# A linear-attention and token-mixing kernel with forty early warm-up matmuls and a new order of all its steps

## The chip, the cores and the metric

The kernel runs on one core of one Trainium2 chip. Its engines, as this text names them: PE (TensorE, matmuls; PEld is its weight load), DVE (VectorE), ACT (ScalarE), POOL (GpSimd) and SP (SyncE, which issues most DMAs). Each takes its instructions strictly in its own order and waits on semaphores for the others. The metric is the device time of one execution in microseconds (us), as the median of several runs. Before the change it is 267.01 us over three runs (266.68 to 268.0).

## The reference

Eight batches of 576 tokens, 8 heads of 64: a linear attention with cosine weights on relu features, and then a mixer over tokens and over channels.

```python
def _attn_ref(q, k, v):                       # 8 x 8 x 576 x 64
    theta = np.pi / 2.0 * pos / S
    def phi(x, c, s):
        r = np.maximum(x, 0.0)
        return np.concatenate([r * c, r * s], axis=-1)
    q_p, k_p = phi(q, cos_w, sin_w), phi(k, cos_w, sin_w)
    kv = np.einsum('bhsf,bhsd->bhfd', k_p, v)
    z = np.sum(k_p, axis=2)
    num = np.einsum('bhsf,bhfd->bhsd', q_p, kv)
    den = np.einsum('bhsf,bhf->bhs', q_p, z)[..., None] + 1e-06
    return num / den
def _moe_ref(x, w_tok1, w_tok2, w_ch1, w_ch2):   # x: 8 x 576 x 512
    h = np.maximum(x.transpose(0, 2, 1) @ w_tok1, 0.0) @ w_tok2
    u = x + h.transpose(0, 2, 1)
    return u + np.maximum(u @ w_ch1, 0.0) @ w_ch2
```

## The kernel before

The whole kernel is a list of small steps, each a function that issues a few instructions (L259 to L742). The program is written out in full; nothing loops on the chip. A letter in a step names its engine: A is ACT, V is DVE, G is POOL, Y is SP.

*Tokens.* The 576 tokens of a batch lie on 128 partitions, four full tiles (j = 0 to 3) and a half-filled fifth (j = 4). The fifth tiles of two batches make one tail tile; the four tails of all batches are the ninth group (g = 8) of the channel mixer.

*Attention of a batch b.* `load` (L274) brings k, q, v. `feat` and `rfeat` (L299, L293) make the relu features in bf16, `vcast` (L309) the bf16 v with a column of ones. `kv` (L598) multiplies features and v on PE, `kv_out` copies the sum to SBUF. q's features are turned: for batches 0 and 1 by PE transposes (`q_turn_mm` L585, 8 matmuls against the identity, and `q_turn_out`, a copy from PSUM), later by DMA (`q_turn` L318, on SP). `num` (L614) multiplies, `x_out` (L621, three DVE instructions) divides and writes x. Batch 0 is done in two halves of four heads (`kv_half`, `num_half`, `x_half` and `b1_half`, L501 to L565).

*Token mixer.* `b1` (L631, two of five matmuls each) and `b1_out` (relu), `u_mm` (L645, two of four matmuls) and `u_out` (L652, DVE, adds x), `u_cast` to bf16 and `u_turn` (L659), a DMA transpose on SP that makes uT. Batch 0 makes its uT on PE instead (`uT_x`, `uT_h`, `uT_out`, L567 to L583). `tail_mm`, `tail_out` and `tail_turn` do the same for two batches' tails.

*Channel mixer of group g.* `m1` (L690) is one of 12 slices of the first layer, four matmuls of 128x512; it needs all of uT. `m1_out` is its relu from PSUM to h1T. The second layer of group 0 is `m2` (L701, 12 steps of four matmuls of 128x512). From group 1 on it is done in a scheme with seven products of half size in place of eight: `h_sum` (L344) makes sums of h1T slices, `prod` (L716, 12 matmuls of 128x256) multiplies, `seed` copies one PSUM bank, `quarter` (L729, DVE) adds to u, and `store` writes out. `w_sum` makes the matching sums of the second weight.

*PSUM.* `take` and `give` (L392, L397) hand out two tiles of two banks (psA, kind "P") and four of one bank (psM, kind "S") in turn. A step that takes a tile waits for whoever read the one before out of it.

*Weights.* `wtok_load`, `wc1_load`, `wc2_load` (L460, L467, L487) bring f32 weights into buffers that are free at that time, and `w1_cast`, `w2_perm`, `w2t_perm`, `wc1_cast`, `wc2_cast` make bf16 copies of them.

*Warm-up.* `warm(n)` (L493) issues n matmuls of 128x512 on zeros (wz, cleared at L411); nothing reads their result.

*Order.* Every step stands in one of the tables ONCE (L21), BATCH (L79) and GROUP (L154) with a place, a number. L749 to L763 add 19 per batch, sort all steps by place and issue them. So the place sets the order in which each engine sees its instructions, the order of SP's DMAs, and who gets which PSUM tile. Batches 3 to 7 and groups 1 to 7 share rows, with some exceptions.

## Time and profile before

| what | value |
|---|---|
| median of 3 runs | 267.01 us (266.68 to 268.0) |
| span of the profiled execution | 265.7 us |
| PE busy | 245.6 us (92% of the span), 2081 matmuls |
| DVE busy | 186.4 us (70%), 360 instructions |
| ACT busy | 135.5 us (51%), 233 instructions |
| POOL busy | 90.1 us (34%), 109 instructions |
| DMA | 57.70 MB, mean 217 GB/s; 380 to 398 GB/s from 7 to 40 us |
| chain of waits | PE 86%, DMA 6%, DVE 3%, SP's queue 1%, ACT 1%, POOL 1% |

The profile is one execution, taken on the chip. Busy time is the time in which an engine had an instruction under way; matmuls overlap in PE's pipeline, so a matmul is listed as longer (379 ns for 128x512) than the distance between two (216 ns). The chain of waits is followed back from the last instruction to what released it, and so on. Over-busy engines off that chain cost nothing by themselves. The first m1 step starts at 33.13 us, the last matmul ends at 261.3 us. Queue times of DMAs: a load of 640 KB lands a median of 5.5 to 8.2 us after its issue, a DMA transpose of qpT 3.4 us, of uT 3.8 us.

### The profile page before, as it was taken

Reading aid. Unit: us, or ns where it says so; the run is one execution under the profiler, and the core shown is the slowest. Engines: PE = TensorE matmul, PEld = TensorE weight load, DVE = VectorE, ACT = ScalarE, POOL = GpSimd, SP = SyncE. Lnnn points to the kernel's source line nnn. Section 1 sums busy time; section 2 is a strip of 40 time slices with the busy share of each in tenths; the row PEclk is TensorE's granted clock in tenths of the full one; section 3 lists DMA queues with packets and bytes.
Section 4 is the critical chain, followed back from the end, with each engine's and each line's share of the span. In section 5 each row is a group of like instructions: output and inputs, shape, how many; then the busy total and the mean of one; then the engine's idle time right before and its main releaser. Section 6 shows DMA issues by size and latency. Waiting matters only on the chain.

```text
span 265.7 us, 5384 instructions
## 1 busy us (share of the span) xinstructions
PE 245.6 (92%) x2081; PEld 158.7 (60%) x2081; DVE 186.4 (70%) x360; ACT 135.5 (51%) x233; POOL 90.1 (34%) x109
## 2 busy tenths in 40 slices
PE   0198999998999999999999999999999999999993
PEld 0176556554448855775487548754875486486482
DVE  4468888969779879778695868587948384256462
ACT  2547678845754387448636863486324402521300
POOL 5064255609634106420460046006600240130340
PEclk9999999999999999999999999999999999999999
DMA  6999999799999899969999999996972043103004
GB/s 195 393 398 386 382 383 368 252 290 152 284 372 157 188 347 336 160 128 317 345 198 128 293 377 182 134 342 221 157 119 121 0 81 148 34 1 158 2 0 159
DMA packets 81754, 57.70 MB, mean 217 GB/s; under 512 B 50240, under 2 KB 76480, under 8 KB 81728
## 3 DMA queue, kind: packets, MB, share of 16 engines
q1 hardware_dynamic: 80768, 56.31, 76.6%
q10 hardware_dynamic: 960, 1.05, 1.3%
q8 instruction: 16, 0.26, 0.4%
q14 instruction: 10, 0.08, 0.1%
HBM read 35.85 MB, written 9.44 MB: 170 GB/s over the span
## 4 chain that ended last, share of the span: by engine, by line
PE 86%; DMA 6%; DVE 3%; SPq 1%; ACT 1%; issue 1%; POOL 1%; DVEq 0%; POOLq 0%
PE psM L694 35%; PE psM L359 26%; PE psA L637 6%; PE psA L649 5%; DMA uT<-u_bf 3%; PE psA L603 3%; DMA v_raw<-in_v_dram 3%; PE psA L617 3%; PE psM L706 2%; PE psM L496 1%; SPq L272 1%; PE psA L676 1%; PE psA L590 1%; PE psM L506 1%; DVE u_sb L653 1%
## 5 line engine op out<-in xcount | busy, mean ns | idle before, releaser
L694 PE MATMUL psM<-uT,w_ch 128*128 128x512 bf16 x384 | 89.9, 379 | 1.4 <-DMA uT<-u_bf 1.4
L287 ACT ACTIVATE h1T<-psM 128x512 bf16<-128x512 f32 x92 | 51.5, 596 | 55.9 <-PE psM L694 54.1
L694 PEld LDWEIGHTS <-w_ch 128*128 128x128 bf16 x432 | 40.5, 98 | 45.4 <-DMA uT<-u_bf 1.8
L283 POOL CAST vb<-v_raw 128x512 bf16<-128x512 f32 (+1 forms) x30 | 20.0, 698 | 70.5 <-DMA v_raw<-in_v_dram 70.5
L359 PEld LDWEIGHTS <-h1s 128*128 128x128 bf16 x384 | 36.7, 98 | 4.9
L371 DVE TENSOR_TENSOR u_sb<-psM,u_sb 128x512 f32<-128x512 f32 x42 | 28.7, 688 | 15.0 <-PE psM L359 14.7
L348 POOL TENSOR_TENSOR h1s<-h1T,h1s 128x512 bf16<-128x512 bf16 (+1 forms) x16 | 21.1, 1318 | 43.9 <-ACT h1T L287 31.3
L359 PE MATMUL psM<-w_ch2t,h1s 128*128 128x256 bf16 x288 | 34.4, 273 | 0.0
L359 PEld LDWEIGHTS <-h1T 128*128 128x128 bf16 x288 | 27.5, 98 | 4.8
L653 DVE TENSOR_TENSOR u_sb<-psA,x_sb 128x1024 f32<-128x1024 f32 x16 | 19.4, 1220 | 12.7 <-PE psA L649 12.5
L305 ACT ACTIVATE kp<-k_raw,sin_t 128x512 bf16<-128x512 f32 x32 | 22.3, 716 | 7.0 <-DMA k_raw<-in_k_dram 5.0
L359 PE MATMUL psM<-w_ch,h1T 128*128 128x256 bf16 x192 | 23.6, 273 | 0.0
L348 DVE TENSOR_TENSOR h1s<-h1T 128x512 bf16<-128x512 bf16 (+1 forms) x24 | 17.5, 728 | 5.5 <-ACT h1T L287 5.4
L305 ACT ACTIVATE kp<-k_raw,cos_t 128x512 bf16<-128x512 f32 x24 | 16.9, 716 | 6.2 <-PE psA L603 5.9
L627 DVE TENSOR_TENSOR x_sb<-psA,rden 128x512 bf16<-128x512 f32 x28 | 19.4, 691 | 1.0
L289 DVE TENSOR_SCALAR h1T<-psM 128x512 bf16<-128x512 f32 x16 | 10.8, 686 | 10.7 <-PE psM L694 10.4
L590 PE MATMUL psM<-ident,qp 128*128 128x128 bf16 x40 | 4.4, 274 | 12.5 <-ACT qp L287 12.5
L617 PEld LDWEIGHTS <-qpT 128*128 128x128 bf16 x280 | 12.3, 98 | 5.5
L649 PE MATMUL psA<-B,w_tok 128*128 128x512 bf16 x64 | 15.6, 379 | 0.0
L283 POOL CAST u_bf<-u_sb 128x1024 bf16<-128x1024 f32 x7 | 9.5, 1359 | 16.3 <-DVE u_sb L653 14.0
L624 DVE TENSOR_SCALAR rden<-psA,eps_t 128x8 f32<-128x8 f32 x35 | 7.8, 223 | 10.3 <-PE psA L617 9.3
L348 POOL TENSOR_TENSOR h1s<-h1T 128x512 bf16<-128x512 bf16 x8 | 10.1, 1261 | 13.3 <-ACT h1T L287 13.3
(114 smaller groups left out, 342.1 us busy)
## 6 DMA issues: line engine op xcount, KB each, us to landing
out_dram<-u_sb SPq DMA_DIRECT2D x32, 256.0 KB, 7.8
q_raw<-in_q_dram SPq DMA_DIRECT2D x8, 640.0 KB, 5.5
k_raw<-in_k_dram SPq DMA_DIRECT2D x8, 640.0 KB, 7.1
v_raw<-in_v_dram SPq DMA_DIRECT2D x7, 640.0 KB, 8.2
q_raw<-in_q_dram SPq DMA_DIRECT2D x8, 512.0 KB, 4.4
k_raw<-in_k_dram SPq DMA_DIRECT2D x7, 512.0 KB, 6.0
v_raw<-in_v_dram SPq DMA_DIRECT2D x7, 512.0 KB, 7.0
u_sb<-in_moe_w_ch_dram SPq DMA_DIRECT2D x2, 1024.0 KB, 10.1
```

The lines of the kernel that those rows point to most:

```text
L283: eng.tensor_copy(out_ap, in_ap)
L287: eng.activation(out_ap, in_ap, AF.Relu)
L305: eng.activation(dst, src, AF.Relu, bias=0.0, scale=s)
L348: eng.tensor_tensor(out=o[:, k0:k1], in0=a[:, k0:k1], in1=b_[:, k0:k1], op=op)
L359: nc.tensor.matmul(bank[:, t * HC:(t + 1) * HC], lhs[:, ki, t * P:(t + 1) * P], rhs[:, ki, :], start=(first and ki == 0 and t == 0), stop= ...
L371: V.tensor_add(u, bank2(bank)[:, ts, :], u)
L617: nc.tensor.matmul(ps[:, h // HH, (h % HH) * E1:(h % HH + 1) * E1], qpT[:, h, j, :], kv_sb[:, h, 0:E1], start=True, stop=True, skip_group_ ...
L627: V.tensor_mul(dst.rearrange("p (g h d) -> p g h d", g=2, h=HH), n[:, :, :, 0:D], bcast(r, [[HH, 2], [1, HH], [0, D]]))
L637: nc.tensor.matmul(ps[:, mi, :], w1[:, j, mi * P:(mi + 1) * P], rhs, start=(j == 0), stop=(j == NJ - 1))
L649: nc.tensor.matmul(ps[:, half, :], w2[:, ki, 2 * c + half, :], B1[b % 2][:, ki, :], start=(ki == 0), stop=(ki == NT - 1))
L653: V.tensor_add(u_sb[b % 2][:, 2 * c:2 * c + 2, :], of(("u", b, c)), x_sb[:, 2 * c:2 * c + 2, :])
L694: nc.tensor.matmul(ps.rearrange("p (t k) -> p t k", k=P), wc1[:, ki, s * P:(s + 1) * P], src[:, :, ki, :], start=(ki == 0), stop=(ki == NC ...
```

## The change

The tables ONCE, BATCH and GROUP and the sort are replaced by one tuple PLAN that lists all 1032 steps in the order in which they are issued. No step of the computation is dropped or added (eight entries of the old tables that issue nothing, tails of even batches, are not listed any more): the same matmuls, copies and DMAs, with the same shapes, are issued in another order, and some on another engine. The memset of wz moves to the front of DVE's program.

Warm-ups: before, 15 matmuls in two steps (3 behind kv_half(0,1), 12 behind num_half(0,2)). After, 20 steps of two: 17 of them stand before the first transpose of batch 0, one right behind it, one before num_half(1,0) and one before the first m1.

Steps by engine, before and after (only kinds that differ):

| kind | ACT | DVE | POOL |
|---|---|---|---|
| m1_out | 92, 70 | 16, 38 | |
| feat | 75, 62 | 45, 58 | |
| rfeat | 8, 15 | 16, 9 | |
| h_sum | | 40, 37 | 24, 27 |
| vcast and vcast_half | 9, 12 | 6, 12 | 30, 21 |
| u_cast | 3, 7 | 4, 1 | 7, 6 |
| wc1_cast and wc2_cast | 2, 4 | 3, 4 | 19, 16 |
| b1_out, kv_out and their halves | 22, 16 | 3, 9 | |
| x_tail and tail_out (of the four tails) | 1, 2 | 3, 2 | 4, 4 |

SP's loads of the head: before k, q, v of batch 0 with v's first part ahead of q's second, then the last third of w_ch1, w_tok, the second third, k and q of batch 1, the first third, v of batch 1. After: q's second part ahead of v, then w_tok, the second third of w_ch1, k of batch 1, the last third, the first third, q and v of batch 1. Then, before, two thirds of w_ch2, k of batch 2, the last third, v and q of batch 2; after, a third of w_ch2, k, the next third, v, q, the last third.

The core of the diff:

```diff
-ONCE = (
-    (-247.4, "load_part", 0, "k", 0, "Y", 0, 8), (-223.9, "load_part", 0, "q", 1, "Y", 0, 8),
-    (-248.1, "load_part", 0, "q", 0, "Y", 0, 8), (-227.5, "load_part", 0, "v", 1, "Y", 0, 4),
-    (-214.7, "load_part", 0, "v", 0, "Y", 0, 4), (-215.8, "load_part", 0, "v", 1, "Y", 4, 8),
-    (-206.9, "load_part", 0, "v", 0, "Y", 4, 8), (-59.4, "warm", 12), (-131.9, "wtok_load"),
-    (-62.9, "wc1_load", 0, 0, 256), (-74.8, "wc1_load", 0, 256, 512), (-100.1, "wc1_load", 1),
-    (-145.1, "wc1_load", 2), (-152.8, "feat", 0, "k", 0, 0, "A"), (-212.5, "feat", 0, "k", 1, 0, "A"),
...
-    (-113.3, "vcast_half", 1, 4, "G"), (-87.2, "kv_half", 0, 4), (-72.2, "kv_half_out", 0, "A"), (-102.3, "warm", 3),
-    (-63.4, "num_half", 0, 0), (-61.2, "x_half", 0, 0, 0), (-59.9, "x_half", 0, 0, 1), (-55.8, "num_half", 0, 1),
...
-BATCH = {}
...
-GROUP = {}
...
+PLAN = (
+    ("load_part", 0, "q", 0, "Y", 0, 8), ("warm", 2), ("warm", 2), ("load_part", 0, "k", 0, "Y", 0, 8),
+    ("feat", 0, "k", 1, 0, "A"), ("load_part", 0, "q", 1, "Y", 0, 8), ("feat", 0, "k", 1, 2, "A"),
+    ("load_part", 0, "v", 1, "Y", 0, 4), ("feat", 0, "q", 1, 4, "A"), ("rfeat", 0, "q", 2, 4, "A"),
+    ("feat", 0, "k", 0, 2, "V"), ("feat", 0, "k", 0, 0, "V"), ("warm", 2), ("warm", 2), ("rfeat", 0, "q", 0, 2, "V"),
+    ("feat", 0, "q", 1, 1, "V"), ("feat", 0, "q", 1, 0, "V"), ("feat", 0, "q", 1, 3, "A"),
+    ("load_part", 0, "v", 0, "Y", 0, 4), ("load_part", 0, "v", 0, "Y", 4, 8), ("load_part", 0, "v", 1, "Y", 4, 8),
+    ("feat", 0, "k", 0, 4, "V"), ("vcast_half", 0, 4, "V"), ("wtok_load",), ("feat", 0, "q", 1, 2, "V"), ("warm", 2),
+    ("warm", 2), ("vcast_half", 1, 1, "G"), ("warm", 2), ("rfeat", 0, "q", 4, 5, "A"), ("warm", 2), ("wc1_load", 1),
+    ("vcast_half", 1, 4, "A"), ("warm", 2), ("warm", 2), ("feat", 0, "k", 0, 3, "V"), ("warm", 2), ("warm", 2),
+    ("warm", 2), ("warm", 2), ("warm", 2), ("warm", 2), ("warm", 2), ("vcast_half", 1, 2, "G"),
+    ("q_turn_mm", 0, 4, "S"), ("vcast_half", 0, 1, "V"), ("warm", 2), ("feat", 0, "k", 1, 1, "A"),
+    ("q_turn_out", 0, 4, "A", "S"), ("vcast_half", 0, 0, "V"), ("kv_half", 0, 0), ("q_turn_mm", 0, 3, "S"),
+    ("feat", 0, "k", 1, 4, "A"), ("w2_perm", 1, "G"), ("feat", 0, "k", 0, 1, "V"), ("feat", 0, "k", 1, 3, "V"),
+    ("load", 1, "k", "Y"), ("vcast_half", 0, 3, "V"), ("kv_half", 0, 1), ("q_turn_mm", 0, 2, "S"),
+    ("q_turn_mm", 0, 1, "S"), ("vcast_half", 0, 2, "V"), ("kv_half", 0, 2), ("kv_half", 0, 3), ("w1_cast", 4, 5, "G"),
+    ("vcast_half", 1, 3, "A"), ("wc1_load", 2), ("w1_cast", 2, 4, "G"), ("w1_cast", 0, 2, "V"),
+    ("q_turn_out", 0, 3, "V", "S"), ("kv_half", 0, 4), ("kv_half_out", 0, "A"), ("wc1_load", 0, 256, 512),
+    ("q_turn_out", 0, 1, "A", "S"), ("vcast_half", 1, 0, "V"), ("kv_half", 1, 0), ("kv_half", 1, 1),
+    ("q_turn_mm", 0, 0, "S"), ("wc1_cast", 3, "G"), ("wc1_cast", 8, "G"), ("q_turn_out", 0, 0, "V", "S"),
+    ("q_turn_out", 0, 2, "A", "S"), ("w2t_perm", 0, "G"), ("num_half", 0, 0), ("kv_half", 1, 2), ("kv_half", 1, 3),
+    ("kv_half", 1, 4), ("kv_half_out", 1, "A"), ("wc1_load", 0, 0, 256), ("wc1_cast", 0, "G"), ("num_half", 0, 2),
+    ("x_half", 0, 0, 0), ("x_half", 0, 0, 1), ("num_half", 0, 1), ("b1_half", 0, 0), ("num_half", 1, 2),
+    ("x_half", 0, 2, 0), ("x_half", 0, 1, 0), ("x_half", 0, 2, 1), ("x_half", 0, 1, 1), ("warm", 2),
+    ("num_half", 1, 0), ("x_half", 1, 0, 0), ("num_half", 1, 1), ("uT_x", 1), ("b1_half", 0, 1), ("x_half", 1, 0, 1),
+    ("load", 1, "q", "Y"), ("x_half", 1, 1, 0), ("b1_half", 0, 2), ("b1_half", 0, 3), ("x_half", 1, 1, 1),
+    ("x_half", 1, 2, 0), ("x_half", 1, 2, 1), ("wc1_cast", 2, "G"), ("wc1_cast", 6, "G"), ("wc1_cast", 5, "V"),
+    ("load", 1, "v", "Y"), ("wc1_cast", 11, "G"), ("b1_half", 0, 4), ("b1_half", 1, 0), ("feat", 1, "k", 0, 2, "V"),
+    ("b1_half", 1, 1), ("b1_half", 1, 2), ("b1_half", 1, 3), ("b1_half_out", 0, "A"), ("b1_half", 1, 4),
+    ("b1_half_out", 1, "V"), ("w2_perm", 0, "A"), ("uT_h", 1), ("uT_x", 0), ("uT_h", 0), ("uT_x", 2),
+    ("wc1_cast", 9, "G"), ("uT_h", 2), ("uT_out", 0, "A"), ("uT_out", 1, "A"), ("feat", 1, "k", 1, 2, "V"),
+    ("uT_out", 2, "A"), ("u_mm", 0, 1), ("w2t_perm", 1, "A"), ("uT_x", 3), ("feat", 1, "k", 0, 3, "A"), ("uT_h", 3),
+    ("uT_out", 3, "A"), ("wc2_load", 0), ("warm", 2), ("wc1_cast", 1, "A"), ("wc1_cast", 10, "G"),
+    ("wc1_cast", 4, "A"),
+
+    ("m1", 0, 5), ("u_mm", 0, 0), ("feat", 1, "k", 1, 1, "A"), ("vcast", 1, 2, "G"), ("u_out", 0, 1), ("m1", 0, 8),
+    ("m1", 0, 1), ("vcast", 1, 0, "G"), ("feat", 1, "k", 0, 0, "V"), ("m1_out", 0, 8, "V"), ("m1_out", 0, 5, "A"),
+    ("m1", 0, 2), ("feat", 1, "k", 0, 1, "V"), ("m1_out", 0, 2, "V"), ("feat", 1, "q", 1, 2, "V"),
+    ("m1_out", 0, 1, "A"), ("m1", 0, 3), ("rfeat", 1, "q", 2, 4, "A"), ("rfeat", 1, "q", 4, 5, "V"),
+    ("feat", 1, "k", 1, 0, "V"), ("feat", 1, "k", 1, 3, "A"), ("load", 2, "k", "Y"), ("feat", 1, "q", 1, 0, "V"),
+    ("m1", 0, 0), ("m1", 0, 6), ("m1_out", 0, 6, "A"), ("feat", 1, "q", 1, 1, "V"), ("m1", 0, 4), ("m1", 0, 11),
+    ("q_turn_mm", 1, 2, "P"), ("vcast", 1, 4, "V"), ("m1_out", 0, 0, "A"), ("u_out", 0, 0),
+    ("rfeat", 1, "q", 0, 2, "A"), ("q_turn_out", 1, 2, "V", "P"), ("m1_out", 0, 4, "A"), ("feat", 1, "q", 1, 4, "A"),
+    ("m1", 0, 9), ("m1_out", 0, 9, "A"), ("q_turn_mm", 1, 1, "P"), ("q_turn_out", 1, 1, "V", "P"),
+    ("q_turn_mm", 1, 4, "P"), ("vcast", 1, 3, "A"), ("wc2_cast", 1, "A"), ("wc1_cast", 7, "G"),
+    ("q_turn_out", 1, 4, "V", "P"), ("q_turn_mm", 1, 0, "P"), ("q_turn_out", 1, 0, "V", "P"),
+    ("feat", 1, "q", 1, 3, "A"), ("m1", 0, 7), ("feat", 1, "k", 1, 4, "A"), ("wc2_cast", 0, "G"),
+    ("q_turn_mm", 1, 3, "P"), ("m1_out", 0, 11, "A"), ("wc2_cast", 2, "G"), ("vcast", 1, 1, "G"),
...
+    ("m2", 0, 3, 1), ("kv", 2, 0), ("kv", 2, 1), ("kv", 2, 2), ("kv", 2, 3), ("m2", 0, 2, 1), ("vcast", 2, 4, "A"),
+    ("kv", 2, 4), ("q_turn", 2, 1), ("b1_out", 1, 0, "A"), ("b1_out", 1, 1, "A"), ("rfeat", 2, "q", 4, 5, "V"),
+    ("u_mm", 1, 0), ("feat", 2, "q", 1, 2, "V"), ("kv_out", 2, "V"), ("feat", 2, "q", 1, 0, "A"),
+    ("wc2_cast", 10, "G"), ("q_turn", 2, 4), ("q_turn", 2, 0), ("rfeat", 2, "q", 2, 4, "A"), ("wc2_cast", 11, "A"),
+    ("u_mm", 1, 1), ("q_turn", 2, 2), ("u_out", 1, 0), ("u_out", 1, 1), ("u_cast", 1, 1, "A"), ("w_sum", 0, "V"),
+    ("u_cast", 1, 0, "G"), ("m2", 0, 0, 2), ("u_turn", 1, 0), ("m2", 0, 3, 2), ("tail_mm", 1),
+    ("feat", 3, "k", 1, 1, "A"), ("m2", 0, 1, 2), ("x_tail", 1, "V"), ("tail_out", 1, "A"), ("num", 2, 1),
+    ("x_out", 2, 1), ("m2_out", 0, 3), ("m2", 0, 2, 2), ("num", 2, 4), ("x_out", 2, 4), ("feat", 3, "k", 0, 2, "A"),
+    ("u_turn", 1, 1), ("w_sum", 2, "G"), ("w_sum", 3, "G"), ("num", 2, 2), ("m2_out", 0, 2), ("load", 3, "q", "Y"),
+    ("m2_out", 0, 0), ("num", 2, 0),
+
+    ("m1", 1, 5), ("m2_out", 0, 1), ("m1_out", 1, 5, "V"), ("w_sum", 1, "V"), ("feat", 3, "k", 0, 0, "A"),
...
+    ("feat", 7, "k", 0, 4, "A"), ("load", 7, "q", "Y"), ("h_sum", 4, 1, 0, 2, "G"), ("m1", 5, 5), ("m1", 5, 3),
+    ("m1_out", 5, 5, "V"), ("prod", 4, 5), ("quarter", 4, 5), ("rfeat", 6, "q", 4, 5, "A"), ("q_turn", 6, 4),
+    ("m1", 5, 0), ("num", 6, 0), ("prod", 4, 3), ("m1_out", 5, 0, "V"), ("x_out", 6, 0), ("feat", 7, "k", 0, 1, "V"),
+    ("feat", 7, "k", 1, 1, "A"), ("quarter", 4, 3), ("m1", 5, 2), ("num", 6, 2), ("m1_out", 5, 3, "A"), ("num", 6, 4),
...
+    ("h_sum", 8, 2, 4, 6, "V"), ("h_sum", 8, 1, 4, 6, "V"), ("prod", 8, 1), ("seed", 8), ("prod", 8, 7),
+    ("h_sum", 8, 2, 0, 2, "G"), ("h_sum", 8, 2, 2, 4, "V"), ("quarter", 8, 7), ("prod", 8, 6),
+    ("h_sum", 8, 1, 0, 2, "G"), ("prod", 8, 4), ("quarter", 8, 6), ("quarter", 8, 4), ("prod", 8, 5),
+    ("quarter", 8, 5), ("store8", 8, 2, 0, 512, "Y"), ("h_sum", 8, 3, 0, 6, "G"), ("prod", 8, 2), ("quarter", 8, 2),
+    ("store8", 8, 3, 0, 512, "A"), ("store8", 8, 0, 0, 256, "A"), ("prod", 8, 3, (0,)), ("prod", 8, 3, (1,)),
+    ("quarter_half", 8, 3, 0), ("store8", 8, 1, 0, 256, "Y"), ("quarter_half", 8, 3, 1),
+    ("store8", 8, 1, 256, 512, "A"), ("store8", 8, 0, 256, 512, "Y"),
+)
...
+    V.memset(wz, 0.0)
     V.memset(raw["k"][:, :, NJ, :], 0.0)
     G.memset(raw["q"][:, :, NJ, :], 0.0)
     load_part(0, "k", 1, A)
     pos_i = sb("pos_i", [P, 1], I32)
     G.iota(pos_i, pattern=[[0, 1]], base=0, channel_multiplier=1)
-    V.memset(wz, 0.0)
...
-    todo = []
-
-    def steps(start, first, rows):
-        for place, fn, *args in rows:
-            args = [engines.get(x, x) for x in args]
-            todo.append((start + place, len(todo), known[fn], [*first, *args]))
-
-    steps(0, (), ONCE)
-    for b in range(1, B + 1):
-        start = 19 * (b - 1)
-        if b < B:
-            steps(start, (b,), BATCH.get(b, BATCH["any"]))
-        steps(start, (b,), GROUP.get(b, GROUP["any"]))
-    for _, _, fn, args in sorted(todo, key=lambda x: x[:2]):
-        fn(*args)
+    for name, *args in PLAN:
+        known[name](*[engines.get(x, x) for x in args])
```

## The prediction, made before the changed kernel was run

> **What bounds the kernel now.** First the busy time of each engine by stretches of the span (columns: stretch and length, then busy us and instructions of PE, PEld, DVE, ACT, POOL, the granted clock, DMA share, GB/s).

> ```profile
> 0.00:13.60 13.60, 1.03 (x8) 0.88 (x9) 5.73 (x27) 5.85 (x10) 3.77 (x18) 1.00 0.87 297
> 13.60:33.10 19.50, 17.72 (x188) 12.63 (x188) 15.35 (x36) 11.87 (x21) 8.19 (x19) 1.00 1.07 388
> 33.10:58.00 24.90, 24.90 (x244) 14.24 (x242) 19.79 (x39) 18.45 (x33) 11.58 (x18) 1.00 0.98 334
> 58.00:66.20 8.20, 7.06 (x61) 3.70 (x60) 7.80 (x15) 3.91 (x6) 6.80 (x4) 1.00 0.93 153
> 66.20:164.50 98.30, 98.30 (x830) 62.90 (x831) 77.15 (x141) 60.34 (x104) 35.38 (x33) 1.00 1.01 254
> 171.00:222.20 51.20, 51.20 (x417) 33.21 (x418) 36.63 (x67) 21.77 (x39) 14.66 (x13) 1.00 0.54 139
> 261.30:265.70 4.40, 0.00 (x0) 0.00 (x0) 0.76 (x2) 0.00 (x0) 0.00 (x0) 0.95 0.52 185
> ```

> PE is busy without a gap from 33.1 on, but for about 1 us around 62; no reordering there can win much. The head is loose: 13.6 us without matmuls, then 19.5 us at 388 GB/s with PE half filled by padding. The chain of waits (start, length, work) shows it:

> ```profile
> 15.95 1.28 PE psM L496 x3
> ...
> 18.55 0.85 PE psM L590 x8
> 19.61 0.45 PE psM L590 x8
> ...
> 21.12 2.59 PE psM L496 x12
> ...
> 24.64 0.70 DVE x_sb L548
> 25.88 0.70 DVE x_sb L548
> ...
> 33.13 2.59 PE psM L694 x12
> ...
> 58.03 0.89 DVE u_sb L653
> ...
> 61.72 4.39 DMA uT<-u_bf
> 66.16 2.76 PE psM L694 x12
> ```

> A warm-up (L496) costs 1.28/3 = 0.427 us at first and 2.59/12 = 0.216 us later; eight transposes (L590) fall from 0.85 to 0.45 between 18.55 and 19.61. So PE runs at half pace until about 19 us (the granted clock reads 1.00 all along and does not show it). The first m1 step starts at 33.13; m1 of group 1 waits for the transposed uT until 66.16.

> **PE's work, which the change keeps.** From chain rows: an m1 or m2 step is 0.86 us (2.59/3), a product 1.31, a batch's kv or num 5 x 0.24, b1 2 x 1.08, u_mm or a tail 0.86. Twelve m1 and twelve m2 of group 0: 20.7. Groups 1 to 8, 12 m1 and 7 products: 8 x 19.5 = 156.3. Seven batches of 6.3: 44.3. Four tails: 3.5. Batch 0 and ten PE transposes: 13.3. Sum 238.1 us without warm-ups. Before, 11.7 of it lies ahead of 33.13, so 33.13 + 226.4 = 259.5; the last matmul ends at 261.3, which leaves 1.8 us of waiting behind the first m1. Then 4.4 us of additions and stores. The new order has 10.3 us ahead of its first m1 (a u_mm and a transpose slip behind it), so, with equal waits later, it breaks even with a first m1 at 33.13 - 1.3 = 31.8.

> **Warm-ups.** 15 become 40; 34 stand ahead of every other matmul and need only wz, whose memset (0.27 us) now is DVE's first, ready at about 1.2. Cold until 7.8 (the 6.5 us that the heating took before, 12.5 to 19), that is 15 x 0.427, then 19 x 0.216: they run from 1.3 to 11.8. The first transpose is ready at 12.9 (below), so they cost nothing and leave PE idle for 1.1 us; if all stayed cold they end at 15.8 and PE starts 2.9 us late. Gone from the path are 3 x 0.427 + 12 x 0.216 = 3.9 us of padding (three steps of 0.43 remain behind the first transpose) and about 2.5 us of half pace (32 kv at 0.055 against 0.031, three transposes at 0.85 against 0.45).

> **The head, step by step.** SP issues q's second part ahead of v (0.26 MB at 388 GB/s: 0.7 us earlier, 10.1) and w_tok ahead of one w_ch1 third (1.05 MB: 2.7 us earlier, 16.2). k still lands at 8.7, v at 13.1.
> - ACT from 8.7: two features (0.62 apart), q at 10.1, a feature, a double relu 0.95, a feature, a relu: 12.9. Then a v cast, a k feature, q_turn_out 0.96, a k feature: 15.6. The last k feature releases kv_half(0,4): 15.9.
> - ACT copies kv out (16.5), q_turn_out(1) to 17.4, q_turn_out(2) to 18.4; DVE ends q_turn_out(0) at 17.85, because PE's transpose 0 waits for the bank that kv_half_out frees. num_half(0,0) runs at 17.9, against 19.8 to 20.1 before.
> - DVE's six x_half (0.35 + 0.69, the small ones 0.35 + 0.42): 18.35 to 23.85. Before they took 20.3 to 27.3, held up by num_half(0,1) behind the 12 warm-ups.
> - b1_half(1,4) 24.1, b1_half_out on DVE behind two copies 25.3; w2_perm(0) on ACT ends 24.4. ACT: three uT_out 25.8 to 27.5, w2t_perm 0.4, a feature 0.62, uT_out(3) to 29.0. First m1: 29.05.
> Moving w1_cast(0,2) to DVE puts a wait for w_tok's landing (14.6 by the sum of bytes) ahead of q_turn_out and x_half; DVE arrives at 14.65. Each us that it is late is a us on the path. With 0.2 us missing at each of ten handovers the first m1 is 31; with q_turn off the path it is 28. I take 29.05. Two forms are in no row: w2_perm(1) on GpSimd (2 x 0.40 by its cast of 128x256, 2 x 0.67 by ScalarE's row: done by 17.6, due at 24.4, hidden) and w2t_perm on ACT (0.38 to 0.62 by casts of like size; 0.4 taken, it stands on the path).

> **Group 0.** PE has 33.2 us from m1(0,5) to m1(1,5). Waits in it: the five transposes of batch 1 now stand close together on two psA tiles (copy out 0.69 on DVE): 0.45; num and x_out of batch 1 on the same two tiles (1.05 per x_out): 0.55; together 1.0, between 0 and 2. Loads: bytes ahead of the last w_ch2 third grow from 15.7 to 18.1 MB, at 360 to 385 GB/s landed at 51 to 53; its cast on ACT stands ahead of u_cast(1,1), which is due at 58, so it is covered by 5 us. On POOL the v casts of batch 2 wait for a load that SP can issue only after batch 1's last v cast near 42, landed by 47; behind them stand the w_ch2 casts 8 to 10, due at 57. Then uT: before, from the end of u_mm(1,0) at 57.8 to m1 at 66.16 there are 8.3 us (two u_out 2.4, cast 1.05, SP's second transpose 4.39). In the new order 6.2 us of PE work stand behind that u_mm: wait 2.1 (before about 1.3). m1(1) starts at 29.05 + 33.2 + 1.0 + 2.1 = 65.35, where before it is 66.16.

> **Engines moved between.** 22 m1_out go from ACT (0.596) to DVE (0.686), 13 features likewise, 7 double relus back. Row means times counts give DVE 203 us in place of 186. DVE is on 3% of the chain, so this is free while each block's PE time covers it: in group 0 DVE has 32 of 33.2 us, in group 5 25.6 of 27.7; elsewhere 1 to 7 us are over. Queues behind SP: q_turn and loads stand earlier against their consumers than before (num 5 to 20 us of PE work behind its features); only q_turn(6,4) follows its relu by 3.5 us where 0.6 + 3.4 are needed: 0.5. Products that wait for a GpSimd h_sum (1.15 to 1.32) keep 0 to 0.3 us. I put the waits behind m1(1) at 0.6, as before; bounds 0.3 and 4.

> **GpSimd apart from VectorE.** The same copy's length varies (minimum/median/maximum in ns):

> ```profile
> L307 DVE TENSOR_SCALAR kp<-k_raw,cos_t x16: 476/478/1137, 8.7 to 170.8; 128x512 bf16<-128x512 f32 x16
> L289 DVE TENSOR_SCALAR h1T<-psM x16: 672/692/693, 35.0 to 252.8; 128x512 bf16<-128x512 f32 x16
> ```

> SBUF to SBUF it reaches 1137, from PSUM it never moves. Over all such rows the excess is about 9 us of DVE time, none of it shown on the path. [...]

> **Sum.** 65.35 + 194.6 + 0.6 + 4.4 = 265.0, against 265.7 of the profiled execution; the median of the runs is 1.3 above that, so 266.2: no change that can be told (0.5%, 1.3 us, is about what can).

> **Rivals.**
> - Full gain: the plan's waits in group 0 are shorter (1 in place of 3.1) and the first m1 comes at 28.5: 28.5 + 33.2 + 1 + 194.6 + 0.4 + 4.4 = 262.1, time 263.4. For it: 9 us are lost in the head. Against: SP still feeds the same bytes at the same rate.
> - Slower: DVE becomes the bound in group 0. It holds 22 more PSUM copies; from PE's point 38 to m1(1) it has 24.0 us of work in 24.2. Decides once its backlog at u_out(1,0) is over 1.4 us: then u_out, cast, transposes and m1(1) are all late by the rest. With 3 us there and 2 more in group 5 the time is 270.5. Against: before, 23.5 of 25.4 in group 1 stalled nothing.
> - The heat doesn't last: between 13 and 18 PE has 4 us of transposes and small matmuls. If the pace halves there, it costs up to half of the 10.3 us, about 2.5 on the path: 268.7. Against: from 24 to 28 PE, busy 3.2 of 4 us, kept 0.055 per transpose. [...]
> [...]

> **Chances.** Forecast 0.42 (a tenth of all it falls below, 0.06 above, 0.26 within 0.5%); full gain 0.27; DVE bound 0.20; heat lost 0.08; contention 0.03. Faster 0.10 + 0.27 + 0.03 = 0.40, same 0.26, slower 0.34. The range 262.5 to 270.5 runs from the full gain with a first m1 at 28 to the DVE case; the forecast's own is 264.3 to 268.

> **What would show it.** Right: warm-ups at 0.427 then 0.216, 34 of them over by 12.5; transposes at 0.45 from the start; first m1 near 29; m1(1) near 65.4 after a wait for uT of 2 us; no PE wait over 0.5 behind it. Wrong: a first m1 after 31 or before 28, DVE without idle time ahead of u_out(1), PE waits for GpSimd's h_sum or q_turn in groups 1 to 6.

## The result: 281.06 us, 5% slower, and the profile after

| kernel | median, us | range | ratio to before, with 95% interval |
|---|---|---|---|
| before | 267.5 | 266.68 to 268.28 | 1 |
| after | 281.06 | 280.79 to 281.9 | 1.0515 [1.0483, 1.0547] |

The ratio here, and each one below, leaves out executions more than 1.5% above the fastest of their kernel (two of b_loads, two of a_heat and one of best2), while medians and ranges are of all. The profiled execution took 280.88 us, its span is 279.1. First the engines' busy time of the kernel after, then the same stretches that the prediction shows of before (stretch and length, busy us and instructions of PE, PEld, DVE, ACT, POOL, granted clock, DMA share, GB/s).

```profile
PE 255.0 (91%) x2092; PEld 159.5 (57%) x2106; DVE 199.0 (71%) x395; ACT 126.9 (45%) x209; POOL 83.1 (30%) x98
```

```profile
0.00:13.60 13.60, 9.87 (x48) 4.34 (x49) 7.23 (x31) 6.75 (x12) 3.91 (x19) 1.00 0.86 302
13.60:33.10 19.50, 17.01 (x189) 11.21 (x189) 13.72 (x36) 12.99 (x23) 7.79 (x14) 1.00 1.07 388
33.10:58.00 24.90, 23.82 (x240) 13.90 (x242) 19.40 (x43) 17.86 (x30) 9.11 (x15) 1.00 1.03 331
58.00:66.20 8.20, 6.25 (x54) 3.33 (x53) 7.20 (x15) 3.52 (x5) 6.93 (x3) 0.95 0.97 164
66.20:164.50 98.30, 91.31 (x740) 55.92 (x744) 74.02 (x144) 53.47 (x89) 23.63 (x22) 0.99 0.93 237
...
171.00:222.20 51.20, 48.37 (x434) 31.81 (x436) 40.81 (x79) 18.28 (x29) 11.87 (x12) 1.00 0.60 155
```

From 66.2 to 164.5 PE was busy for all of the 98.3 us before, and 830 matmuls were done; after, 7 us of idle time have come in and 740 are done. The chain of waits (start, length, work) gives the two marks of the forecast:

```profile
27.82 0.86 PE psM L755 x4
...
61.64 3.13 DMA uT<-u_bf
64.82 4.46 PE psM L755 x12
```

The first m1 starts at 27.8 (before 33.1), m1 of group 1 at 64.8 (before 66.2). Up to there the kernel is ahead. Then the waits of PE behind the first m1, from a list of the whole span (engine, tile, line, releaser: us, times, longest), of after and then of before:

```profile
PE psM L755 <- DMA uT<-u_bf: 2.5, 3, 1.4
PE psA L678 <- DMA qpT<-qp: 2.3, 3, 1.8
PE psA L698 <- ACT B L348: 2.1, 3, 0.7
PE psA L678 <- DVE x_tl L688: 1.3, 1, 1.3
...
PE psA L678 <- DVE qp L368: 1.0, 1, 1.0
...
PE psA L698 <- DVE B L350: 0.8, 1, 0.8
PE psA L678 <- DVE x_sb L688: 0.8, 3, 0.4
PE psM L755 <- ACT h1T L348: 0.7, 1, 0.7
PE psA L710 <- DVE B L350: 0.6, 2, 0.3
```

```profile
PE psM L694 <- DMA uT<-u_bf: 1.4, 2, 1.1
```

Before, PE waited for one thing behind its first m1, uT. After, it waits for twelve, of which the nine longest in total stand here. The list counts idle time only. Counted as the distance between the starts of matmuls less their pace (0.216 us for 128x512 and so on, which adds to each wait the 0.16 us by which the 0.379 us of a listed matmul outlast that pace), the sum closes:

| term | us |
|---|---|
| first m1 at 27.8 in place of 33.1 | -5.3 |
| useful work of PE ahead of it: 10.3 in place of 11.65 | +1.35 |
| waits from first m1 to m1 of group 1: 3.8 in place of 1.3 | +2.5 |
| waits behind that: 15.25 in place of 0.4 | +14.9 |
| sum (spans: 279.1 - 265.7 = 13.4) | +13.4 |

The 15.25 us by kind (half clock is the time lost while the granted clock of PE was 0.5): num for a transposed qp tile 4.00 (0.51, 1.93, 0.38 and 1.18; the list books the last under a VectorE feature that ended within 0.05 us of that transpose's landing); b1's second step for the relu of its first 3.47 (four times 0.84 to 0.94); m1 for uT 2.52; m1 for a PSUM tile 1.42; b1 for x_out 1.31; u_mm for b1's relu 0.87; half clock 1.66. None is for a GpSimd h_sum. Two of them in PE's timeline, in their last columns the idle time and its releaser:

```profile
125.78 0.42 PE L678 MATMUL psA<-kv_sb,qpT 128*128 128x65 bf16 x8 [1.76 <-DMA qpT<-qp]
...
131.54 0.38 PE L698 MATMUL psA<-x_tl,w_tok 128*128 128x512 bf16 x1
132.60 1.02 PE L698 MATMUL psA<-x_sb,w_tok 128*128 128x512 bf16 x4 [0.68 <-ACT B L348]
```

What the late transposes have in common stands in SP's timeline, here ahead of the wait at 125.78:

```profile
117.44 1.29 SPq L333 DMA_DIRECT2D q_raw<-in_q_dram  x2
118.78 5.85 SPq L380 DMA_TRANSPOSE qpT<-qp  x2
```

All four transposes of qp, and the two of uT behind which m1 waited 0.84 and 1.52 us, were issued behind the load of a q or a v with no other work of SP between, but for one more transpose in two cases. The four of qp landed 6.7 to 7.7 us after their issue, where the median before is 3.4. Together these six waits are 6.4 of the 15.25 us.

The change's other aim, GpSimd apart from VectorE, was met in part. The same copies as the prediction shows of before (minimum, median, maximum in ns):

```profile
L368 DVE TENSOR_SCALAR kp<-k_raw,cos_t x22: 472/479/653, 8.5 to 186.0; 128x512 bf16<-128x512 f32 x22
...
L350 DVE TENSOR_SCALAR h1T<-psM x38: 678/683/692, 30.6 to 266.6; 128x512 bf16<-128x512 f32 x38
```

The longest of these copies from SBUF fell from 1137 to 653 ns, while those from PSUM stay within 14 ns (21 before). In the two profiles all five of the copies from SBUF that took over 500 ns (615 to 1137) ran beside an instruction of GpSimd, and the 33 that met none took 472 to 488. Over all instructions that read SBUF alone, the time over the shortest of the same line and shape fell from 11.4 to 9.3 us on VectorE and from 9.6 to 5.1 on GpSimd: some 6.6 us of engine time. PE could not win much by it, since it waited 1.7 us in all behind its first m1 before, and for uT alone.

### The profile page after: what moved, and what is told of

It is laid out like the page before. It is cut to its first block, busy times and chain, and to the rows that moved or that the text cites. A ratio compares the mean times of both kernels' runs of the same rounds, so it can differ in the third digit from the quotient of the medians.

```text
span 279.1 us, 5401 instructions
## 1 busy us (share of the span) xinstructions
PE 255.0 (91%) x2092; PEld 159.5 (57%) x2106; DVE 199.0 (71%) x395; ACT 126.9 (45%) x209; POOL 83.1 (30%) x98
## 3 DMA queue, kind: packets, MB, share of 16 engines
q10 hardware_dynamic: 960, 1.05, 1.3%
## 4 chain that ended last, share of the span: by engine, by line
PE 51%; DVE 16%; issue 12%; DMA 11%; SPq 3%; ACT 3%; POOL 1%; DVEq 0%; POOLq 0%; ACTq 0%
PE psM L755 20%; PE psM L420 16%; DMA q_raw<-in_q_dram 5%; PE psA L698 4%; DMA qpT<-qp 4%; PE psA L710 4%; DMA uT<-u_bf 3%; DVE x_sb L688 3%; PE psA L664 2%; PE psM L767 2%; SPq L380 1%; DVE qp L368 1%; PE psA L678 1%; SPq L333 1%; DVE u_sb L714 1%
## 5 line engine op out<-in xcount | busy, mean ns | idle before, releaser
L755 PE MATMUL psM<-uT,w_ch 128*128 128x512 bf16 x384 | 93.7, 384 | 3.4 <-DMA uT<-u_bf 2.5
L348 ACT ACTIVATE h1T<-psM 128x512 bf16<-128x512 f32 x70 | 40.1, 595 | 71.7 <-PE psM L755 63.2
L432 DVE TENSOR_TENSOR u_sb<-psM,u_sb 128x512 f32<-128x512 f32 x42 | 28.6, 687 | 20.6 <-PE psM L420 20.3
L350 DVE TENSOR_SCALAR h1T<-psM 128x512 bf16<-128x512 f32 x38 | 25.7, 685 | 14.0 <-PE psM L755 7.6
L409 POOL TENSOR_TENSOR h1s<-h1T 128x512 bf16<-128x512 bf16 (+1 forms) x15 | 20.3, 1363 | 21.3 <-DVE h1T L350 19.6
L344 POOL CAST vb<-v_raw 128x512 bf16<-128x512 f32 (+1 forms) x21 | 13.7, 672 | 36.0 <-DMA v_raw<-in_v_dram 36.0
L678 PEld LDWEIGHTS <-qpT 128*128 128x128 bf16 x280 | 12.5, 98 | 13.1 <-DMA qpT<-qp 4.9
L366 ACT ACTIVATE kp<-k_raw,sin_t 128x512 bf16<-128x512 f32 x24 | 16.9, 718 | 4.9 <-DMA k_raw<-in_k_dram 4.9
L678 PE MATMUL psA<-kv_sb,qpT 128*128 128x65 bf16 x280 | 13.9, 193 | 5.4 <-DMA qpT<-qp 2.3
L348 ACT ACTIVATE qp<-q_raw 128x1024 bf16<-128x1024 f32 (+1 forms) x15 | 14.4, 968 | 7.9 <-DMA qpT<-qp 5.5
L698 PE MATMUL psA<-x_sb,w_tok 128*128 128x512 bf16 x49 | 14.0, 378 | 3.8 <-ACT B L348 2.1
L409 DVE TENSOR_TENSOR h1s<-h1T,h1s 128x512 bf16<-128x512 bf16 (+1 forms) x20 | 16.4, 825 | 0.3
```

The lines of the kernel that those rows point to most:

```text
L344: eng.tensor_copy(out_ap, in_ap)
L348: eng.activation(out_ap, in_ap, AF.Relu)
L350: eng.tensor_relu(out_ap, in_ap)
L409: eng.tensor_tensor(out=o[:, k0:k1], in0=a[:, k0:k1], in1=b_[:, k0:k1], op=op)
L432: V.tensor_add(u, bank2(bank)[:, ts, :], u)
L678: nc.tensor.matmul(ps[:, h // HH, (h % HH) * E1:(h % HH + 1) * E1], qpT[:, h, j, :], kv_sb[:, h, 0:E1], start=True, stop=True, skip_group_ ...
```

## The experiments

Ratios are to runs of the kernel before on the same chip. "Old" and "new" are the orders before and after.

**One part of the change undone in the new order.** b1swap issues b1's second step ahead of the first one's relu (batches 4 to 7), m1back gives every m1_out its old engine:

```diff
 # b1swap
-    ("b1", 5, 0), ... ("b1_out", 5, 0, "A"), ("b1", 5, 1),
+    ("b1", 5, 0), ... ("b1", 5, 1), ("b1_out", 5, 0, "A"),
 # m1back (44 steps)
-    ("m1_out", 1, 5, "V"),
+    ("m1_out", 1, 5, "A"),
```

> The new order, but for batches 4 to 7 the second b1 step is issued ahead of the relu of the first (b1(b,1) before b1_out(b,0)). Theory 'placement' (the lost time is a sum of local waits, because PE's steps stand directly behind what frees their tile or makes their input): PE waited 0.84, 0.85, 0.94 and 0.84 us for this relu, 3.47 in all; the waits go and the time falls by 2.5 to 3.5 us. Rival 'VectorE late' (VectorE carries 22 more relus and everything that ends on it comes late, so another wait takes over): less than 1 us.

Measured 279.34 (278.48 to 280.33), ratio 1.0454 [1.0412, 1.0497]: 1.7 us less than the new kernel, about half of what the waits held. The waits at b1 went. For batches 5 and 7, 0.86 and 0.75 us came back one step on, where u_mm waits for the second relu, and a wait for uT of 0.83 is new near 205.

> The new order, but every m1_out runs on the engine that it had before (44 steps change: 33 go back from VectorE to ScalarE, 11 the other way). Rival 'VectorE late': VectorE loses about 15 us of work, PE's waits for x_out, u_out and the features shrink, the time falls by 5 us or more. Theory 'placement': the order stays as tight as it is; between 2 us faster and 3 us slower.

Measured 281.91 (279.68 to 282.63), 1.0522 [1.046, 1.0583]: no gain. Giving VectorE's 22 relus back does not free the new order. But the waits did not stay as they were: one of b1 for x_out grew from 0.28 to 1.80 us, and a product now waits 1.18 us for a relu on ScalarE. What the relus cost there is thus not shown.

**The same parts put into the old order.** There PE waits for almost nothing, so that a part's cost stands bare.

```diff
 # b_b1tight (batches 4 to 7)
-    ("b1", 5, 0), ("m1", 4, 9), ("b1_out", 5, 0, "A"), ("m1", 4, 10), ("b1", 5, 1),
+    ("b1", 5, 0), ("b1_out", 5, 0, "A"), ("b1", 5, 1), ("m1", 4, 9), ("m1", 4, 10),
 # b_loads (batches 4 to 6)
+    ("load", 5, "q", "Y"), ("load", 5, "v", "Y"),
     ("q_turn", 4, 2), ... ("u_turn", 3, 0), ("u_turn", 3, 1), ... ("q_turn", 4, 4), ...
-    ("load", 5, "q", "Y"), ("load", 5, "v", "Y"),
 # b_m1out (44 steps): the engine of every m1_out as in the new kernel
```

> The order of before, with one part of the new order put in for batches 4 to 7: the relu of the first b1 step, then the second b1 step, directly behind the first, with no work of PE between. Theory 'placement': the second step waits for the relu's read of the tile that it shares, 0.85 us as in the new kernel, four times: 3.4 us slower than before. Rival 'several things are late at once' (a wait at b1 only takes the place of one that stands behind it): under 1.5 us slower.

Measured 270.56 (269.93 to 271.31), 1.0142 [1.0107, 1.0177]: 3.6 us slower, as the first theory has it. Its list of waits has one line that before's has not:

```profile
PE psA L680 <- ACT B L330: 2.7, 4, 0.7
```

The second step writes the other one of the tile's two banks, and still stands until ScalarE has read the first. Whether the chip asks for this, or only the semaphores that the tile brings with it, no run shows.

> The order of before, with one part of the new order put in for batches 4 to 6: SP issues the loads of the next batch's q and v (2.36 MB, some 6 us at 390 GB/s) ahead of the last two transposes of qp and of both transposes of u_bf, in place of behind them. Theory 'placement': num and the next group's m1 wait for late transposes, 1 to 3 us a batch, 3 to 8 us slower in all. Rival (the transposes have slack enough): under 1 us slower.

Measured 285.54 (281.01 to 286.93), 1.0599 [1.0512, 1.0686]: far over the expected. PE's timeline, then two windows (of an execution at the long end of that range):

```profile
119.95 0.42 PE L660 MATMUL psA<-kv_sb,qpT 128*128 128x65 bf16 x8 [4.07 <-DMA qpT<-qp]
```

```profile
120.20:123.70 3.50, 3.50 (x21) 2.22 (x18) 0.00 (x0) 0.00 (x0) 0.58 (x2) 0.51 0.99 258
```

The transpose landed at 119.9 in place of 113.6 us. Of these 6.3 us, 4.0 passed before it was issued, while SP issued the four DMAs of the two loads, and 2.3 on the longer way: the last part of v landed at 118.9, the transpose 1.0 behind it. In this trace, as in those of all other kernels here, SP's 144 DMAs land in the order in which they were issued. PE waited for such a transpose three times, 12.8 us of idle time in all, and behind each wait it ran at a clock of 0.5 for 3.4 or 6.8 us, which had not been thought of.

> The order of before, but every m1_out on the engine that it has in the new kernel (44 change: 33 to VectorE, 11 to ScalarE). Rival 'VectorE late': over 4 us slower than before. Theory 'placement': under 2 us slower, since PE's work between the steps covers it.

Measured 273.82 (273.2 to 274.67), 1.0266 [1.0232, 1.0299]: 6.9 us slower. Here the rival is right. Waits that before has not:

```profile
PE psA L660 <- DVE x_tl L670: 1.8, 2, 1.0
PE psM L402 <- POOL h1s L391: 1.5, 1, 1.5
...
PE psA L719 <- DVE u_sb L696: 0.6, 1, 0.6
```

A wait of 1.9 us for uT at 92.8 is new too. So these relus' engines cost much in the old order, and returning them gains nothing in the new one.

**Engines against order.** b_engines is the old order with all of the new kernel's engines (218 steps differ), a_engines the reverse.

> The order of before with the engines of the new kernel: every step that may run on several engines takes the one it has there (218 steps change letter, the order of the steps stays that of before). Theory 'the new engines are the load' (m1_out alone cost 6.9 us there): 273 to 277, six to ten us over before. Theory 'the new order is the load': under 3 us over before, that is under 270. Both may hold; then it is m1_out's cost and little else.

> The new order with the engines of before (the same 218 steps changed back). Theory 'the new engines are the load': most of the 14 us comes back, under 274. Theory 'the new order is the load': 279 to 290, no better or worse than the new kernel, since its places were chosen for its engines.

Measured 308.49 (307.29 to 310.04), 1.153 [1.1475, 1.1585], and 317.62 (316.39 to 319.15), 1.1862 [1.1795, 1.1929]. Both theories miss. The costliest waits behind the head, of b_engines and then of a_engines:

```profile
PE psM L737 <- ACT h1T L330: 9.8, 2, 5.0
PE psA L646 <- POOL vb L326: 5.0, 1, 5.0
```

```profile
PE psA L683 <- DVE x_sb L673: 6.4, 5, 3.0
PE psM L405 <- DVE h1s L394: 4.7, 4, 3.5
```

Part of the loss is in the head, where the first m1 came at 39.8 and 42.4 us. Each order holds only with its own engines: the moves between engines and the places in the order can't be priced apart by these two runs.

**SP's order undone in the new kernel.** a_qturn moves seven transposes ahead of the next load of q; a_loads also puts the loads of q and v as late as their first readers allow; a_three is a_loads with b1swap and m1back.

```diff
 # a_qturn
+    ("q_turn", 4, 1), ("q_turn", 4, 2),
     ("load", 5, "q", "Y"), ...
-    ("q_turn", 4, 2), ("q_turn", 4, 1),
```

> The new order, but with SP's queue turned back where a load stood ahead of transposes: for batches 4 to 6 the last transposes of qp go ahead of the next batch's loads of q and v, and those loads stand as late as their first reader allows. Theory 'SP's order' (b_loads cost 18.6 us in the old order by this alone): PE's waits for qpT (0.51, 1.93, 0.38, and 1.18 behind a late q) and part of those for uT (0.84, 1.52) go: 3 to 5 us faster than the new kernel, 276 to 278. Theory 'late in several places at once': the features of the later loaded q and v, the b1 steps and VectorE are late too, under 1.5 us faster.

> The new order with three parts undone together: the loads as in a_loads, the b1 steps as in b1swap, the engines of m1_out as in m1back. Theory 'late in several places at once': each alone gave little because another wait stood behind it, together they give more than the sum of the three alone: 6 us or more faster than the new kernel, 275 or less. Rival 'independent': the sum of the three, with a_loads' own gain, -1.7 and +0.9.

> The new order with only the transposes moved: for batches 3 to 5 those transposes of qp that stood behind the next batch's load of q go ahead of it; the loads of v stay where they were (a_loads, 294.0, had moved them behind, and PE then waited 5.9 us for kv). Theory 'first in, first out' (a transpose lands behind whatever bytes were issued before it): the waits for qpT of 1.93 and 0.38 at 124 and 128 us go, 1.5 to 3 us faster, 278 to 279.5. Rival (SP then waits for the features and holds up the loads): no gain, 281 or more.

Measured 294.02 (292.4 to 294.74), 295.89 (293.98 to 298.33) and 289.93 (289.64 to 291.64): 13, 15 and 9 us slower than the new kernel, where the theories had a gain, or none at best. Only the rival of a_qturn, "no gain, 281 or more", holds, and its reason in part: the loads were held up, though by SP's time for issuing the transposes more than by a wait for features. The two transposes landed at 121.8 and 120.6 in place of 125.7 and 128.1, and PE's wait for them is gone. VectorE's timeline shows what took its place:

```profile
122.28 0.69 DVE L417 TENSOR_TENSOR u_sb<-psM,u_sb 128x512 f32<-128x512 f32 x1
127.03 0.43 DVE L335 TENSOR_SCALAR qp<-q_raw 128x512 bf16<-128x512 f32 x1 [4.07 <-DMA q_raw<-in_q_dram]
```

The new order has the features of batch 5's q on VectorE ahead of x_out of batch 4. Now the load of q is the one that lands late, VectorE stands 4.07 us before it (2.02 in the new kernel), and PE waits 3.2 us for x_out behind it. The longest wait of PE is a second one:

```profile
157.85 5.06 PE L740 MATMUL psM<-uT,w_ch 128*128 128x512 bf16 x12 [5.12 <-DMA uT<-u_bf]
```

SP issued this transpose of u_bf at 151.6 in place of 142.9 us, behind the four transposes of batch 5 and the load of q that the edit had put ahead of it. At each of the two waits the clock fell to 0.5 for 6.8 us. In a_loads the late load is that of v, issued at 118.9 in place of 109.4 us: ScalarE stands 11.6 us before a v cast of batch 5 that the new order has ahead of kv_out of batch 4. PE waits 5.7 us for that kv_out and 6.8 for one h_sum on GpSimd; a_three has both waits too (4.8 and 4.3), so that undoing three parts together helps no more than one. The transposes' waits are thus no slip in SP's order that can be undone alone: the readers of the loads were moved up as well. Since each of the three edits also made waits of its own, they do not show what the order of loads and transposes costs in the new kernel.

**Where the loss sits: the new order up to a point, the old from there.** headA_restB has 147 steps of the new order, a299_restB 299 (to the last m2 steps of group 0). The seam is the place where one order ends and the other begins.

> The first 147 steps of the new order (all 40 warm-ups, batch 0 up to its transposed uT, ahead of the first m1), then all other steps in the order of before. Theory 'placement': the head keeps its gain (first m1 near 28 in place of 33.1), and before's rest has 1.8 us of waits behind it: 27.8 + 227.8 + 1.8 + 4.4 = 261.8 of span, time about 263, some 4 us under before. Rival 'the early head collides' (loads of w_ch2 and batch 1 arrive no sooner, so group 0 waits for what the head gained): 266 to 268.

Measured 271.07 (269.84 to 271.64), 1.0138 [1.0097, 1.0178]. The seam spoiled it. VectorE's timeline, then PE's:

```profile
31.53 0.87 DVE L352 TENSOR_SCALAR qp<-q_raw,tan_t 128x512 bf16<-128x512 f32 x1 [5.06 <-DMA q_raw<-in_q_dram]
```

```profile
34.60 1.01 PE L635 MATMUL psA<-ident,qp 128*128 128x128 bf16 x8 [6.01 <-DVE u_sb L698]
```

VectorE stood before q's features with u_out behind them, since q of batch 1 lands at 31.4 in the new order of loads. The clock then stood at 0.5 for 6.8 us. After that PE's only wait over 0.3 us is one of 0.77 for uT.

> The first 299 steps of the new order (the head and group 0 up to the last m2 steps), then the order of before. The new kernel waited for no v, k or q in this stretch, so the seam should not cost what it did with 147 steps. Theory 'placement': first m1 at 27.8, 1.4 us of waits in group 0, a wait for uT of about 2, m1 of group 1 at 64 to 65, then 0.4 us of waits: span 263 to 264, time 264 to 265.5, under before by 2 us. Rival (what the new order does in group 0 leaves a backlog that the later groups pay for): 267 or more.

Measured 266.28 (265.77 to 266.57), 0.9977 [0.9965, 0.9989]: 14.8 us under the new kernel, and the rival's backlog did not come. The first 299 steps are as good as the old ones, so the loss sits in the steps behind them. At the seam PE waited 1.80 and 0.86 us for x_out, with two w_sum of VectorE ahead of it.

best1 and best3 move what stood there (w_sum, one transpose and one num), and best2 mends the other seam.

> The kernel a299_restB (266.28) with three moves around m1 of group 1: VectorE's two w_sum behind x_out(2,0), the transpose of qp tile 2 of batch 2 behind both transposes of u_bf, and its num behind the third m1 step. There PE waited 1.8 and 0.86 us for VectorE, which had 2.9 us of w_sum ahead of x_out, and SP issued uT 2.1 us late behind that transpose. Theory 'local waits': m1 of group 1 starts 1.5 to 2.5 us earlier, time 264 to 265. Rival (the next wait is right behind): within 0.5 us of 266.3.

> a299_restB with uT of group 1 brought forward as in best1 (m1 of group 1 started at 63.43 there, against 65.03 and 66.16), and the two w_sum that stood on VectorE ahead of x_out and m2_out put back as before has them: the first on GpSimd, the second on VectorE behind the last m2_out. Theory 'local waits': best1's waits of 1.82, 1.14 and 0.88 us behind VectorE go, m1 of group 1 at 63.4, span 263 to 264, time 264.3 to 265.4. Rival: another wait of VectorE's in group 1 takes their place, 266 or more.

> The first 150 steps of the new order (the head), then before's order with the seam mended: headA_restB lost 6.2 us because VectorE stood before the features of q of batch 1 (landed at 31.4) ahead of u_out of batch 0, and 2.5 us of half clock behind that wait. Here u_out(0,.), u_mm(0,0) and six m1 steps with their relus go ahead of those features. Theory 'the head is sound': first m1 at 27.7, no wait over 1 us in group 0 but that for uT, time 262 to 264. Rival (group 0 now runs into the weights and loads, whose landing has not moved): 265 to 267.

best1: 268.12 (267.7 to 270.38), 1.0068 [1.0039, 1.0098]. best3: 268.86 (268.01 to 269.49), 1.009 [1.0068, 1.0112]. m1 of group 1 came at 63.4 and 63.7 as expected, and 3 to 6 us later the waits began that took the gain: in best1 1.82 us for m2_out and 1.14 and 0.88 for x_out, in best3 2.47 for x_out, all on VectorE. The rivals were right. best2: 265.68 (264.89 to 270.09), 0.9932 [0.9899, 0.9965], as its rival has it. Its only trace is of the execution of 270.09 us, so where the head's gain went in the others is not shown.

**Warm-ups alone.** before_warm is the old order with 34 warm-ups at the front and no padding, warm2 has 44 and three pairs more among the first matmuls.

> The order of before, with 34 warm-ups ahead of PE's first transpose and without the 15 padding matmuls; the memset of wz is VectorE's first. Theory 'padding and half pace cost before': PE's 3.9 us of padding and 2.5 us of half pace go, of which VectorE's x_half chain hides some: first m1 at 30 to 31, time 264 to 265. Rival 'the head hangs on loads and features, not on PE': first m1 stays within 0.5 us of 33.1 and the time within 1 us of before.

> The order of before with 44 warm-ups ahead of the first transpose and three pairs between the first matmuls of batch 0. In before_warm (34, none between) the granted clock fell to 0.5 from 14.2 to 21.0, after PE had idled from 10.1 to 12.6. Theory 'the heat must be held': the clock stays at 1.0, first m1 0.5 to 1.5 us before 32.2, time 263.5 to 264.8. Rival (by then the chain runs through VectorE and ScalarE, not PE): within 0.5 us of 265.2.

before_warm: 265.24 (265.09 to 265.93), 0.9934 [0.9911, 0.9956]; the first m1 came at 32.2, between the two forecasts, so most of the 6.4 us that went from PE were hidden. Its windows:

```profile
10.00:14.20 4.20, 1.06 (x18) 0.89 (x18) 2.37 (x7) 3.54 (x7) 0.94 (x2) 1.00 1.07 400
14.20:21.00 6.80, 6.08 (x86) 5.92 (x84) 4.76 (x11) 3.56 (x7) 3.50 (x9) 0.50 1.05 394
```

warm2 kept the clock at 1.0 there and was no faster: 266.16 (265.78 to 266.87), 0.9973 [0.9956, 0.999], first m1 at 31.8. There PE waited 0.68 us for VectorE's x_half and 1.48 for ScalarE's relu of b1 ahead of the first m1, so the head hangs on these more than on PE's pace.

**The half clock.** In the new kernel the clock fell right behind the wait for uT:

```profile
62.20:65.40 3.20, 1.39 (x19) 0.89 (x19) 3.13 (x7) 0.44 (x1) 3.12 (x2) 1.00 0.86 148
65.40:68.80 3.40, 3.40 (x10) 1.18 (x8) 2.81 (x6) 0.00 (x0) 0.68 (x1) 0.50 0.98 313
```

> The new kernel with four more pairs of warm-ups in the idle time of PE ahead of m1 of group 1 (62.5 to 64.8). In the profile of the new kernel the granted clock fell to 0.5 from 65.4 to 68.8, right behind that idle time, and m1 ran at half pace there. Theory 'the clock falls for idle time': the clock stays at 1.0, 1 to 1.7 us faster than the new kernel (281.06). Rival (the window that fell was decided by the work before, or the pairs stand in the way): within 0.5 us of it, or slower.

Measured 281.77 (279.44 to 284.28), 1.0532 [1.0498, 1.0566]: no gain. The clock held at 65 us, but m1 of group 1 began 0.7 us later, at 65.5, and the clock fell at 125.3 instead, behind a wait for qpT that had grown from 1.76 to 2.75 us:

```profile
125.30:128.70 3.40, 3.06 (x15) 1.42 (x16) 2.23 (x6) 0.00 (x0) 0.00 (x0) 0.50 1.03 334
```

## Why the prediction was wrong

- **Up to m1 of group 1 it was close.** First m1 29.05 forecast, 27.8 measured, just under the 28 that it had named as a sign of being wrong; waits in group 0 3.1 and 3.8; m1 of group 1 65.35 and 64.8, so that two errors partly cancel. The last x_half ended at 23.7 (23.85 forecast); the steps from there to the first m1 took 4.2 us, not 5.2.
- **Warm-ups.** Of the right kind, mis-sized: they ran from 1.2 to 10.1 in place of 1.3 to 11.8, as the clock came after 2.8 us, not 6.5 (2.7 to 5.9 in the profiles of the other kernels whose warm-ups begin at 1.2). The transposes began at 12.6 and ran at full pace (0.46 us for eight). before_warm shows that this part alone is worth 0.7%.
- **The step that failed** is the one line "I put the waits behind m1(1) at 0.6, as before; bounds 0.3 and 4". They were 13.6 us and 1.7 of half clock. It took over the waits of the old order. b1's two steps, with the relu between them and no work of PE, were not looked at (3.5 us; b_b1tight has 3.6 for the same in the old order, b1swap gives back 1.7). Of SP's queue, only q_turn(6,4) was priced, at 0.5, with the median flight before of 3.4 us: behind a load it took 6.7, and the wait was 1.18. q_turn(3,3), (4,2) and (4,1) were called early enough: behind their loads they took 7.0 to 7.7 us, and the waits were 2.82. The margin can be measured: the 30 num steps of turned tiles start 0.36 us or more behind the landing of their transpose before, with one under 0.5; after, five are under 0.5, four of these at 0.04 or 0.05.
- **VectorE as the bound** was a rival at 0.20 and 270.5. b_m1out puts its price at 6.9 us in the old order, more than the 5 assumed; in the new order its price is not shown (m1back gained nothing). That VectorE is free at 3% of the chain of waits did not carry over: after the change it has 16% of it, and PE 51% in place of 86%.
- **The heat** (the full clock) was placed wrong: the clock was at 1.0 from 3.98 to 65.42, so also from 13 to 18, where a loss of 2.5 us was feared, and fell behind a wait at 62 to 65.
- **GpSimd.** That its h_sums keep the products waiting by no more than 0.3 us held: PE never waited for one. What the separation from VectorE is worth by itself no run shows, nor that contention between the two, given a chance of 0.03, made the 1.8 us of waits: the profiles show longer copies beside GpSimd's instructions (827 and 1137 ns in place of 478), and PE's waits behind its first m1 before for uT alone.
- **Open.** Of the parts put into the old order alone, b1's steps cost what their waits hold, and the relus and the loads cost more than expected; taken out of the new order, a part gives back half (b1) or nothing (m1_out), or costs more (loads). Which set of moves would free the new order was not found. Not tried: two separate PSUM tiles for b1's halves; a load moved together with all of its readers.

The best of all kernels here are before_warm and best2, 0.7% under before.

## What to carry to other kernels

When an order is replaced whole, do not ask only whether each engine's load fits: list for every cross-engine handover (transpose to matmul, relu to the next write of its tile, load to its first reader) how much work of the bounding engine lies between, and doubt each one under a microsecond (b1's four without any work between cost 0.84 to 0.94 us each). Transposes issued behind a load in the same queue were late by what the load took to be issued and to land (6.3 us for 2.36 MB in b_loads), and a reader put early held up all behind it on its engine (VectorE for 4.07 us in a_qturn, ScalarE for 11.6 in a_loads). Undoing one suspect in a tight schedule says little; putting it alone into the loose one gives its price there.

## What the runs showed of the hardware

```
PE busy share    next window at 0.5    next window at 1.0
under 0.45              25                    0
0.45 to 0.52             3                    9
over 0.52                0                 1467
```

In these profiles, once at 0.5, windows with a busy share of up to 0.79 were followed by another at 0.5, those from 0.80 on by 1.0. Waits of 2 us within one such window were thus enough to lose a further 1.7 us, half of the next window (new kernel, 62.0 to 65.4 and 65.4 to 68.8). A window without work of PE was not needed: this one had PE busy for 0.43 of the time.
